# Spreading a chunk's row scatters over the steps of the expert blocks, in a causal-convolution and mixture-of-experts kernel on one core

## The chip, the cores and the metric

The kernel runs on one core of one Trainium2 chip. The core has five engines that run side by side and wait for each other by semaphores: TensorE (PE in the profile, with its weight loads as PEld), VectorE (DVE), ScalarE (ACT), GpSimd (POOL) and SyncE (SP, which here only issues transfers). Sixteen DMA engines move the data. The metric is the time of one execution on the device in microseconds (us).

## The reference

Two stages, one after the other, over 28672 tokens (8 sequences of 3584) of 192 numbers each:

```python
# 1: a causal filter of 7 taps, its weights a softmax, one filter for each of 8 groups of 24 columns
out = np.einsum('hk,bskhg->bshg', softmax(weight), x_unf)
x = out.reshape(28672, 192)

# 2: every token goes to the one expert of 8 that its direction fits best
logits = (x / |x|) @ (expert_emb / |expert_emb|).T / tau
e, gate = argmax(logits), its softmax probability
out[token] = gate * (np.maximum(x[token] @ w1[e], 0) @ w2[e])     # 192 -> 1024 -> 192
```

## The kernel before

The tokens are worked on in 16 **chunks** of 1792 (112 partitions by 16 columns). For a chunk, `mix` computes the filter on TensorE and the norms; `route` cuts the result into a high and a low half in 16 bits, transposes it by DMA (`turn`, L503), computes the logits and the expert of each token, and gives every token a place `di` in its expert's region of a table `rows_d` in DRAM. Then it writes the chunk's rows there with 16 indirect transfers of 112 rows, issued by GpSimd (`scatter`, L507), one for each column.

The experts' work is done in **blocks** of at most 512 tokens of one expert (`expert`, L653). SP loads a block's rows transposed (`fetch`, L632, up to three blocks ahead). VectorE copies the expert's weights into `slot` (L611 to L618). For each eighth of the hidden layer TensorE makes five matmuls into `h_ps` (L672), ScalarE writes the relu's high part (L674) and VectorE the low part (L675) into `hid`. Then, for each 128 tokens, 24 matmuls go into `o_ps` (L692), ScalarE scales the result by the gate into `y` (L696), and GpSimd scatters y to the output by token number (L697). `expert` is a generator: it yields once after each piece of the hidden layer and once after each y. These are the **steps**: twelve for a block of 512, eight and four.

`hand_out` makes blocks of the rows that are surely complete; it is called ahead of the chunks in `PICK` (2, 3, 5, 8, 12), and a block's loads wait for all scatters that had been issued by then (`need`). `last_blocks` does so at the end, after `pads` has scattered nine transfers of padding rows.

`dispatch` is a generator too: it runs `mix` and `route` of the chunks, up to two mixes ahead, and each yield states how much VectorE and ScalarE time it used. `run` ties the two together: after each step of a block it credits what VectorE and ScalarE have left beside TensorE (times `rate`, which `hand_out` sets so that the next hand-out comes `LEAD` before the blocks run out), and pulls pieces from `dispatch` while there is credit. Chunks 0 and 1 are worked on while the weights are prepared; chunks 2 to 15 run beside the blocks; after chunk 15 only blocks are left.

This order of the program is what the scheduler starts from. It orders the instructions of each engine by that priority and by when they are ready; SP alone keeps the written order. GpSimd executes its queue in order, and the scatters of a chunk and the y's of the blocks are in the same queue. The pools that touch them: `rows` has two buffers, `out` (y) four.

Of the kernel before, what the change touches and what calls it, by code (L numbers as in the profile page):

```python
# [16 lines left out]
AF = mybir.ActivationFunctionType  # L17
# [13 lines left out]
NT = 16  # L31
# [20 lines left out]
LEAD = 26.0  # L52

CAP = 6.0


def _dep(tc, frm, to, sync=True):
    cls = mybir.DependencyClass.Sync if sync else mybir.DependencyClass.NoSync
    tc.add_manual_dep(
        frm, to, mybir.DependencyInfo(cls, mybir.DependencyReason.DATA),  # L60
        reason="routed rows are written before they are read",
    )


class _Moe:
    def __init__(self, ctx, tc, x, weight, emb, tau, w1, w2, out):
        self.tc, self.nc = tc, tc.nc
        self.x, self.weight, self.emb, self.tau = x, weight, emb, tau
        self.w1, self.w2, self.out = w1, w2, out
        B, S, _ = x.shape  # L70
        self.B, self.S, self.N = B, S, B * S
        self.nch = self.N // CT
        self.per_b = S // CT
        self.cap = self.N + PAD
        self.dummy = E * self.cap
        pool = lambda name, bufs, **k: ctx.enter_context(
            tc.tile_pool(name=name, bufs=bufs, **k))
        self.cp = pool("const", 1)
        self.xp = pool("xload", 2)
        self.rp = pool("rows", 2)  # L80
        self.xtp = pool("xtrans", 2)
        self.sp = pool("small", 2)
        self.lp = pool("lone", 1)
        self.ep = pool("expert", 3)
        self.yp = pool("y", 3)
        self.op = pool("out", 4)
        self.mp = pool("meta", 8)
        self.rings = {k: pool("ps_" + k, n, space=PSUM)
                      for k, n in (("r", 2), ("l", 1), ("h", 5))}

        self.res = self.cp.tile([128, E * RES], F16, name="res")
        self.slot = self.cp.tile([128, S2 + RES - W2], F16, name="slot")
        self.hid = self.cp.tile([128, 2 * NFC * 512], F16, name="hid")
        self.dp = pool("scratch", 1, space=DRAM)
        self.rows_d = self.dp.tile([E * self.cap + PAD, RW], I32, name="rows_d")
        self.scatters = []
        self.xts, self.mixed = [], {}
        self.weights_in, self.later = False, []
        self.subs, self.ready, self.at, self.copied = [], 0, 0, 0
# [277 lines left out]
    def route(self, c, xbar):  # L377
        xTs = []
        nc, sp = self.nc, self.sp
        xc, s, si, f = self.mixed.pop(c)  # L380
        r32 = self.rp.tile([TP, NT, RW], I32, tag="rows", name="rows")
# [4 lines left out]
        for g in range(0, NT, GX):  # L386
# [7 lines left out]
                out=rows[:, u, 256:384], in0=xc[:, u, 0:128],  # L394
                in1=rows[:, u, 0:128], op=ALU.subtract)
            nc.vector.tensor_tensor(
                out=rows[:, u, 192:256], in0=xc[:, u, 128:192],
# [17 lines left out]
        for g in range(NT // GX):  # L415
            if xbar:
                xT = xTs[g]
            else:
                xT = self.xtp.tile([128, GX, 3, TP], F16, tag="xT", name="xT")
                for k in range(3):  # L420
                    tp = self.ps("r", [128, GX, TP], F16, "tr_ps")
                    for a in range(GX):
                        nc.tensor.transpose(
                            out=tp[:, a, :],
                            in_=rows[:, g * GX + a, k * 128:(k + 1) * 128],
# [3 lines left out]
            for a in range(GX):  # L429
                for k in range(3):  # L430
                    nc.tensor.matmul(  # L431
                        out=lg[:, g * GX + a, :], lhsT=xT[:, a, k, :],
# [7 lines left out]
            out=l, in_=lg.rearrange("p t (k e) -> p t e k", k=2), op=ALU.add,  # L440
# [3 lines left out]
        m = sp.tile([TP, NT], F32, tag="m", name="m")  # L444
# [12 lines left out]
            out=l, in0=l, scalar=0.0, op0=ALU.is_equal,  # L457
# [32 lines left out]
        self.dve = nc.vector.tensor_single_scalar(  # L490
            out=di, in_=dr, scalar=-1.0, op=ALU.add).ins
        yield 0.8, 0.0
        for t in range(NT):
            self.scatter(di[:, t:t + 1], r32[:, t, :])
            if t % 2:
                yield 0.3, 0.3
        self.left += CT


    def turn(self, rows, t, n):  # L500
# [152 lines left out]
    def expert(self):  # L653
        nc, tc = self.nc, self.tc
        while self.ready < min(self.at + 3, len(self.subs)):
            self.fetch()
        u, xT, mt, T = self.subs[self.at][3:]
        self.copy_w1(self.at)
        self.at += 1
        nj = T // 128  # L660
        w1 = lambda b, c: self.slot[:, b + c * 128:b + (c + 1) * 128]
        w2 = self.slot[:, S2:S2 + WS - W2].rearrange("p (c d) -> p c d", d=2 * D)
        hh, hl = (self.hid[:, i * NFC * T:(i + 1) * NFC * T].rearrange(
            "p (c t) -> p c t", t=T) for i in range(2))

        m = 512 // T
        for b in range(0, NFC, m):
            ps = self.ps("h", [128, m, T], F32, "h_ps")
            for c in range(m):
                for i, (o, k) in enumerate(  # L670
                        ((0, 0), (0, 2), (F, 0), (2 * F, 1), (3 * F, 1))):
                    nc.tensor.matmul(out=ps[:, c, :], lhsT=w1(o, b + c),  # L672
                                     rhs=xT[:, k, :], start=(i == 0), stop=(i == 4))
            nc.scalar.activation(out=hh[:, b:b + m, :], in_=ps, func=AF.Relu)  # L674
            nc.vector.scalar_tensor_tensor(  # L675
                out=hl[:, b:b + m, :], in0=ps, scalar=0.0, in1=hh[:, b:b + m, :],
                op0=ALU.max, op1=ALU.subtract)
            if b == (0 if m > 2 else 2 if m == 2 else 1) and u == 0:
                self.copy_w2()
            yield self.slack(512)  # L680
        self.copy_w1(self.at)

        g = self.yp.tile([128, 4], F32, tag="g", name="g")
        nc.vector.tensor_scalar(
            out=g[:, 0:nj], in0=mt[:, :, 1].bitcast(F32),
            scalar1=self.slot[:, S2 + WS - W2:S2 + WS - W2 + 2].bitcast(F32), scalar2=None, op0=ALU.mult)
        for a in range(nj):
            o = self.ps("h", [128, D], F32, "o_ps")
            q = slice(a * 128, (a + 1) * 128)
            for c in range(NFC):  # L690
                for i, (h, k) in enumerate(((hh, 0), (hh, D), (hl, 0))):
                    nc.tensor.matmul(out=o, lhsT=h[:, c, q], rhs=w2[:, c, k:k + D],  # L692
                                     start=(c + i == 0),
                                     stop=(c == NFC - 1 and i == 2))
            y = self.op.tile([128, D], F32, tag="y", name="y")
            nc.scalar.activation(out=y, in_=o, func=AF.Copy, scale=g[:, a:a + 1])  # L696
            i = nc.gpsimd.indirect_dma_start(  # L697
                out=self.out[:, :],
                out_offset=bass.IndirectOffsetOnAxis(ap=mt[:, a, 0:1], axis=0),
                in_=y, in_offset=None, bounds_check=self.N - 1,  # L700
                oob_is_err=False).ins
            tc.declare_no_dep(i, group="out", reason="tokens are distinct")
            tc.add_to_no_dep_group("out", i)
            yield OUT
# [16 lines left out]
    def dispatch(self, first, ring):  # L721
        a = b = ()
        na = nb = 0
        da = db = 0.0
        last = first if ring == "h" else self.nch
        share = AHEAD if ring == "h" else 1.0
        ca, cb = (0, 0) if ring == "h" else (first, first)
        a, b = None, None
        while cb < last:
            if b is None and cb in self.mixed:  # L730
                if ring != "h" and cb in PICK[1:]:
                    self.hand_out(cb)
                b, db = self.route(cb, ring != "h"), 0.0
            if a is None and ca < min(last, cb + 2):
                a, da = self.mix(ca, ring, first), 0.0
            if a is not None and (b is None or da * COST_B <= db * COST_A * share):
                v = next(a, None)
                if v is None:
                    a, ca = None, ca + 1
                    continue  # L740
                da += sum(v)
            else:
                v = next(b, None)
                if v is None:
                    b, cb = None, cb + 1
                    continue
                db += sum(v)
            yield v
# [25 lines left out]
    def run(self):  # L774
# [14 lines left out]
        a = self.dispatch(first, "h")  # L789
# [15 lines left out]
        a = self.dispatch(first, "r")  # L805
        for _ in range(PRE):
            next(a)
        live, due, done = next(a, None), [0.0, 0.0], False
        while live or not done or self.at < len(self.subs):
            if self.at < len(self.subs):  # L810
                for v in self.expert():
                    due = [min(CAP, d + self.rate * t) for d, t in zip(due, v)]
                    while live and min(due) >= 0.0:
                        due = [d - t for d, t in zip(due, live)]
                        live = next(a, None)
            elif live:
                live = next(a, None)
            if not live and not done:
                self.last_blocks()
                done = True  # L820
        order.__exit__(None, None, None)
# [19 lines left out]
```

## Time and profile before

| | |
|---|---|
| Median of 3 runs | 1531.99 us (1530.37 to 1540.09) |
| The profiled execution | 1535.34 us |
| Its span, first to last instruction | 1533.5 us |
| Mean granted clock of TensorE | 0.878 |
| Busy: PE, PEld, DVE, ACT, POOL | 1227.3, 917.6, 847.0, 575.5, 538.5 us |
| Indirect transfers on POOL: rows, y, padding | 256, 231, 9 |

Lines of the page and of the answers are read so: a group has its line in the kernel, engine, operation, what it writes and reads, and its count, then busy time and the mean in ns of one, then how long the engine stood idle just before these instructions and what ended most of that. A line with forty digits cuts the span into 40 slices of 38.3 us; a digit is the busy share in tenths, or for PEclk the clock that TensorE was granted. A line that begins with a stretch (200.90:234.90) gives its length and, for each engine, busy time and the count of instructions, then granted clock, the DMA engines' share and GB/s. A line of the timeline has start, duration, engine, line and operation, and in brackets the idle time before it and what ended that. "remote" and "another core or an unknown queue" stand for a semaphore whose update the profile could not put down to an instruction that ended near it. Ends of matmuls are modelled.

### The profile page before, as it was taken

The page shows a single profiled execution, that of the slowest core. Times are in us where ns is not written, and L with a number is a line of the kernel's source. Part 1 is how long each engine was busy: PE and PEld are TensorE (multiplying, and loading weights), DVE is VectorE, ACT ScalarE, POOL GpSimd, SP SyncE. Part 2 cuts the span into 40 slices and gives each one's busy share as a digit, 9 for nine tenths or more (in the row PEclk, how much of TensorE's full clock was granted, in tenths as well). Part 3 has the DMA queues.
Part 4 walks back from the last instruction along what each step waited for, and adds up shares of the span by engine and source line. Part 5 has one row for each costly group of instructions (what it writes and reads, how often), then busy time and mean ns, then how long its engine had stood idle before and what let it go on. Part 6 is the DMA issues. An engine that isn't in the chain of part 4 may idle for free.

```text
span 1533.5 us, 28412 instructions
## 1 busy us (share of the span) xinstructions
PE 1227.3 (80%) x10460; PEld 917.6 (60%) x10460; DVE 847.0 (55%) x2162; ACT 575.5 (38%) x1335; POOL 538.5 (35%) x564
## 2 busy tenths in 40 slices
PE   4745768877968677798696969595899999998997
PEld 2533647665647454455473647373577767778787
DVE  3945857656537456375562627253555465547745
ACT  3834525524342323353343325131333333333332
POOL 0044255355343433533524242526222222222222
PEclk9656979878879788797898979797899999999999
DMA  9334463455315254254362523332122112211210
GB/s 257 103 102 137 101 141 94 94 125 125 82 47 119 55 130 105 77 126 102 79 132 57 124 66 61 78 61 77 32 53 48 43 35 49 53 37 41 56 37 24
DMA packets 273228, 129.07 MB, mean 84 GB/s; under 512 B 215054, under 2 KB 263565, under 8 KB 273088
## 3 DMA queue, kind: packets, MB, share of 16 engines
q1 hardware_dynamic: 249280, 80.39, 24.7%
q0 software_dynamic: 23808, 46.87, 10.1%
q8 instruction: 82, 1.34, 0.4%
q14 instruction: 58, 0.48, 0.1%
HBM read 38.35 MB, written 47.53 MB: 56 GB/s over the span
## 4 chain that ended last, share of the span: by engine, by line
PE 62%; another core or an unknown queue 9%; issue 7%; DVE 4%; ACT 3%; DMA 3%; SPq 2%; POOL 0%; POOLq 0%; DVEq 0%; ACTq 0%
PE h_ps L672 28%; PE o_ps L692 28%; PE conv_ps L344 5%; ACT hid L674 2%; SPq L503 2%; PE lg_ps L431 2%; DMA xT<-rows 2%; DMA xt<-in_dram 2%; DVE hid L675 1%; DVE slot L617 1%; ACT sq L354 1%; ACT rows L391 0%; DVE slot L611 0%; ACT xt L347 0%
## 5 line engine op out<-in xcount | busy, mean ns | idle before, releaser
L692 PE MATMUL o_ps<-slot,hid 128*128 128x192 f16 x5544 | 546.7, 255 | 155.9 <-issue 94.7
L692 PEld LDWEIGHTS <-hid 128*128 128x128 f16 x5544 | 479.3, 101 | 218.9 <-issue 144.7
L672 PE MATMUL h_ps<-e_xT,slot 128*128 128x512 f16 (+2 forms) x3520 | 556.5, 312 | 46.5 <-DVE hid L675 29.5
L697 POOL DMA_INDIRECT out_dram<-y,e_mt x231 | 259.0, 1121 | 728.2 <-ACT y L696 654.3
L675 DVE SCALAR_TENSOR_TENSOR hid<-h_ps,hid 128x512 f16<-128x512 f32 x462 | 313.5, 687 | 296.6 <-ACT hid L674 215.0
L672 PEld LDWEIGHTS <-slot 128*128 128x128 f16 x3520 | 311.8, 100 | 240.3 <-issue 70.7
L674 ACT ACTIVATE hid<-h_ps 128x512 f16<-128x512 f32 x462 | 271.1, 597 | 430.4 <-PE h_ps L672 236.7
L507 POOL DMA_INDIRECT rows_d<-rows,di x256 | 258.0, 1008 | 181.9 <-issue 99.8
L696 ACT ACTIVATE y<-o_ps,g 128x192 f32<-128x192 f32 x231 | 91.4, 419 | 342.9 <-PE o_ps L692 212.7
L617 DVE COPY slot<-res 128x3074 f16 x82 | 79.9, 975 | 185.5 <-PE o_ps L692 110.7
L344 PE MATMUL conv_ps<-xt,band 128*112 128x384 f32 x256 | 116.7, 567 | 39.9 <-DMA xt<-in_dram 35.0
L347 ACT COPY xt<-conv_ps 112x384 f32<-112x384 f32 x128 | 60.8, 479 | 116.1 <-PE conv_ps L344 84.8
L611 DVE COPY slot<-res 128x3072 f16 x82 | 78.5, 958 | 40.6 <-remote 37.0
L431 PEld LDWEIGHTS <-xT 128*112 128x112 f16 x768 | 67.6, 149 | 47.1 <-DMA xT<-rows 17.1
L344 PEld LDWEIGHTS conv_ps<-xt,band 128*112 128x112 f32 x256 | 45.7, 202 | 63.5 <-issue 44.9
L431 PE MATMUL lg_ps<-ma,xT 128*112 128x16 f16 x512 | 67.0, 202 | 18.3 <-DMA xT<-rows 11.5
L354 ACT ACTIVATE sq<-xt 112x192 f32<-112x192 f32 x192 | 67.9, 356 | 4.8 <-DVE sq L357 2.3
L389 DVE TENSOR_TENSOR xt<-xt,x_p_s 112x768 f32<-112x768 f32 x64 | 58.2, 950 | 0.0
L431 PE MATMUL lg_ps<-mb,xT 128*112 128x16 f16 x256 | 50.1, 206 | 8.7 <-ACT xT L427 5.7
L391 ACT CAST rows<-xt 112x768 f16<-112x768 f32 x64 | 50.6, 829 | 12.2 <-DVE xt L389 7.5
L357 DVE SCALAR_TENSOR_TENSOR sq<-xt 112x192 f32<-112x192 f32 x64 | 22.6, 354 | 57.5 <-ACT sq L354 56.6
L393 DVE TENSOR_TENSOR rows<-xt,rows 112x512 f16<-112x512 f32 x64 | 43.6, 682 | 2.1 <-DMA out_dram<-y,e_mt 1.2
(157 smaller groups left out, 543.3 us busy)
## 6 DMA issues: line engine op xcount, KB each, us to landing
xt<-in_dram SPq DMA_DIRECT2D x8, 1536.0 KB
xt<-in_dram SPq DMA_DIRECT2D x8, 1440.0 KB
rows_d<-rows,di POOLq DMA_INDIRECT x256
out_dram<-y,e_mt POOLq DMA_INDIRECT x231
xT<-rows SPq DMA_TRANSPOSE x224
hid<-in_dram SPq DMA_DIRECT2D x3, 768.0 KB
slot<-in_dram SPq DMA_DIRECT2D x3, 768.0 KB
hid<-in_dram SPq DMA_DIRECT2D x3, 512.0 KB
```

Source lines behind the costliest of these rows:

```text
L344: nc.tensor.matmul(out=ps, lhsT=self.band[:, h, :], rhs=xt[:, :, h * G:(h + 1) * G], start=True, stop=True)
L354: nc.scalar.activation(out=sq, in_=xc[:, t, :], func=AF.Square, accum_out=n2[:, t:t + 1])
L431: nc.tensor.matmul(out=lg[:, g * GX + a, :], lhsT=xT[:, a, k, :], rhs=self.mb if k == 1 else self.ma, start=(k == 0), stop=(k == 2))
L507: i = self.nc.gpsimd.indirect_dma_start(out=self.rows_d[:, :], out_offset=bass.IndirectOffsetOnAxis(ap=idx, axis=0), in_=src, in_offset=No ...
L611: nc.vector.tensor_copy(out=self.slot[:, 0:W2], in_=v)
L617: self.nc.vector.tensor_copy(out=self.slot[:, S2:], in_=self.res[:, bass.ds(self.we + W2, RES - W2)])
L672: nc.tensor.matmul(out=ps[:, c, :], lhsT=w1(o, b + c), rhs=xT[:, k, :], start=(i == 0), stop=(i == 4))
L674: nc.scalar.activation(out=hh[:, b:b + m, :], in_=ps, func=AF.Relu)
L675: nc.vector.scalar_tensor_tensor(out=hl[:, b:b + m, :], in0=ps, scalar=0.0, in1=hh[:, b:b + m, :], op0=ALU.max, op1=ALU.subtract)
L692: nc.tensor.matmul(out=o, lhsT=h[:, c, q], rhs=w2[:, c, k:k + D], start=(c + i == 0), stop=(c == NFC - 1 and i == 2))
L696: nc.scalar.activation(out=y, in_=o, func=AF.Copy, scale=g[:, a:a + 1])
L697: i = nc.gpsimd.indirect_dma_start(out=self.out[:, :], out_offset=bass.IndirectOffsetOnAxis(ap=mt[:, a, 0:1], axis=0), in_=y, in_offset=No ...
```

## The change

`route` no longer issues a chunk's scatters. It appends the 16 of them to a list, `pend`, and the main loop issues them with `put`: after two of every three steps of the blocks one scatter, with a dependency on the step's ScalarE instruction (the relu of L674 or the y of L696). There are exceptions. Ahead of a hand-out, `dispatch` puts out all that is pending, without a dependency. After the last chunk, one goes out after each step, also without one, and `last_blocks` comes when none is left. In the chunks 0 and 1, worked on with the weights, the scatters go out in `route` as before. A new route is begun only while at most 16 scatters are pending; until then `dispatch` yields a piece of 0.5 without work, if it has no mix to do either.

```diff
+SPREAD = 3
...
         yield 0.8, 0.0
-        for t in range(NT):
-            self.scatter(di[:, t:t + 1], r32[:, t, :])
-            if t % 2:
-                yield 0.3, 0.3
+        self.pend += [(di[:, t:t + 1], r32[:, t, :]) for t in range(NT)]
+        while self.pend and not xbar:
+            self.put()
+            yield 0.15, 0.15
         self.left += CT
+
+
+    def put(self, step=None):
+        if self.pend:
+            self.scatter(*self.pend.pop(0))
+            if step is not None:
+                _dep(self.tc, self.scatters[-1], step.name)
...
-            nc.scalar.activation(out=hh[:, b:b + m, :], in_=ps, func=AF.Relu)
+            self.step = nc.scalar.activation(
+                out=hh[:, b:b + m, :], in_=ps, func=AF.Relu).ins
...
-            nc.scalar.activation(out=y, in_=o, func=AF.Copy, scale=g[:, a:a + 1])
+            self.step = nc.scalar.activation(
+                out=y, in_=o, func=AF.Copy, scale=g[:, a:a + 1]).ins
...
-            if b is None and cb in self.mixed:
+            if b is None and cb in self.mixed and len(self.pend) <= NT:
                 if ring != "h" and cb in PICK[1:]:
+                    while self.pend:
+                        self.put()
+                        self.put()
+                        yield 0.3, 0.3
                     self.hand_out(cb)
...
+            elif b is None:
+                v = 0.5, 0.5
             else:
...
-        live, due, done = next(a, None), [0.0, 0.0], False
-        while live or not done or self.at < len(self.subs):
+        live, due, done, steps = next(a, None), [0.0, 0.0], False, 0
+        while live or self.pend or not done or self.at < len(self.subs):
             if self.at < len(self.subs):
                 for v in self.expert():
+                    steps += 1
+                    if not live and not done:
+                        self.put()
+                    elif steps % SPREAD:
+                        self.put(self.step)
...
-            elif live:
-                live = next(a, None)
-            if not live and not done:
+            else:
+                self.put()
+                if live:
+                    live = next(a, None)
+            if not live and not done and not self.pend:
                 self.last_blocks()
                 done = True
```

More of the change, by code (lines that the diff above doesn't have):

```diff
@@ L95, in __init__ @@
         self.rows_d = self.dp.tile([E * self.cap + PAD, RW], I32, name="rows_d")
-        self.scatters = []
+        self.scatters, self.pend, self.step = [], [], None
         self.xts, self.mixed = [], {}
```

## The prediction, made before the change was run

> **What bounds the kernel now.** I read the slices of the page first, then its groups, then windows of busy time laid around each chunk's scatters.
>
> ```profile
> PE   4745768877968677798696969595899999998997
> POOL 0044255355343433533524242526222222222222
> PEclk9656979878879788797898979797899999999999
> ...
> PE 62%; another core or an unknown queue 9%; issue 7%; DVE 4%; ACT 3%; DMA 3%; SPq 2%; POOL 0%; POOLq 0%; DVEq 0%; ACTq 0%
> ...
> L692 PE MATMUL o_ps<-slot,hid 128*128 128x192 f16 x5544 | 546.7, 255 | 155.9 <-issue 94.7
> L672 PE MATMUL h_ps<-e_xT,slot 128*128 128x512 f16 (+2 forms) x3520 | 556.5, 312 | 46.5 <-DVE hid L675 29.5
> L697 POOL DMA_INDIRECT out_dram<-y,e_mt x231 | 259.0, 1121 | 728.2 <-ACT y L696 654.3
> L507 POOL DMA_INDIRECT rows_d<-rows,di x256 | 258.0, 1008 | 181.9 <-issue 99.8
> ```
>
> TensorE (PE) carries the kernel: the blocks' matmuls at L692 and L672 are 1103 of its 1227 us. From slice 29 on, where no chunk is left, it is full at full clock. Before that its digits and the granted clock dip where POOL's digit rises. So I laid 34 us windows from the first scatter of each chunk. These are the nine chunks (3, 5, 6, 8, 9, 10, 12, 13, 14) whose scatters the change gates; columns are length, then busy time of PE, its weight loads, DVE, ACT and POOL, then granted clock, DMA share and GB/s.
>
> ```profile
> 250.30:284.30 34.00, 23.23 (x197) 17.44 (x195) 16.51 (x43) 8.04 (x21) 22.50 (x22) 0.85 0.63 151
> 359.10:393.10 34.00, 22.70 (x156) 15.91 (x154) 15.75 (x44) 9.09 (x28) 18.57 (x18) 0.75 0.55 134
> 413.20:447.20 34.00, 20.58 (x111) 11.19 (x109) 8.35 (x13) 6.63 (x13) 19.39 (x20) 0.75 0.26 72
> 560.70:594.70 34.00, 19.16 (x137) 12.44 (x136) 10.74 (x27) 11.15 (x37) 19.06 (x20) 0.75 0.23 62
> 621.80:655.80 34.00, 22.66 (x145) 14.07 (x144) 10.60 (x27) 9.52 (x36) 20.06 (x22) 0.70 0.24 69
> 680.30:714.30 34.00, 25.73 (x167) 16.65 (x166) 16.01 (x43) 10.29 (x36) 21.05 (x22) 0.75 0.31 86
> 801.70:835.70 34.00, 20.01 (x118) 11.80 (x117) 8.05 (x14) 8.21 (x16) 18.06 (x20) 0.80 0.27 65
> 873.90:907.90 34.00, 19.33 (x109) 11.49 (x107) 8.11 (x17) 5.98 (x13) 19.05 (x20) 0.75 0.29 78
> 964.80:998.80 34.00, 17.23 (x94) 9.36 (x92) 5.72 (x10) 5.33 (x11) 19.25 (x20) 0.66 0.30 74
> sum 306.00, PE 190.62 PEld 120.36 DVE 99.84 ACT 74.24 POOL 176.98; mean PE 21.18 PEld 13.37 DVE 11.09 ACT 8.25 POOL 19.66
> ```
>
> The thirteen stretches between the bursts (their sum, and one of them) and the block-only tail look quite different:
>
> ```profile
> 393.10:413.20 20.10, 20.10 (x169) 14.30 (x168) 15.69 (x40) 10.40 (x21) 4.95 (x7) 1.00 0.21 37
> sum 396.80, PE 384.74 PEld 294.47 DVE 291.63 ACT 200.72 POOL 86.61; mean PE 29.59 PEld 22.65 DVE 22.43 ACT 15.44 POOL 6.66
> 1100.00:1500.00 400.00, 382.39 (x3761) 301.65 (x3759) 225.17 (x387) 138.33 (x270) 102.65 (x95) 1.00 0.20 46
> ```
>
> Between bursts PE is busy 384.74 of 396.80 us (97%), with the same mixing and routing beside the blocks; in the tail 96%. Nearly all that PE loses in the middle of the kernel, it loses while a chunk's 16 scatters run. That no engine's own work causes this shows in the timeline of chunk 14's burst:
>
> ```profile
> 960.57 8.08 PE L692 MATMUL o_ps<-slot,hid 128*128 128x192 f16 x96
> ...
> 976.01 0.94 POOL L507 DMA_INDIRECT rows_d<-rows,di  x1 [0.30 <-DMA rows_d<-rows,di]
> 977.94 1.01 DVE L617 COPY slot<-res 128x3074 f16 x1 [13.90 <-remote]
> 977.99 0.42 ACT L696 ACTIVATE y<-o_ps,g 128x192 f32<-128x192 f32 x1 [10.60 <-remote]
> ```
>
> The last of these matmuls should have ended at 968.65, yet the copy of w2 and the fourth y, which both wait for it, start together at 977.9, DVE having stood for 13.90 us. Meanwhile POOL issues without a stop: 0.94 us and 0.30 of idle, one scatter in 1.24 us. PE's completions come late as long as POOL runs back to back. By what path one holds up the other no row tells.
>
> The Trainium skill, SBUF — State Buffer, section "Who interferes with whom", states that PE and ACT never wait on anyone. By it the scatters could not hold PE and spreading them would give nothing; the late release at 977.9 does not agree, but it is counted as a rival below.
>
> **What the change does, and the price of the gap.** Sixteen scatters a chunk no longer go out at once: in two of three steps (a relu or a y) one goes, and it waits for that step's ACT instruction. No transfer is removed or added; the waits are semaphore instructions of 17 ns on POOL (shortest and median; the longest is a real wait). Five bursts stay: those flushed ahead of the hand-outs (chunks 2, 4, 7, 11; the first and the last are shown), and chunk 15 with the nine pad scatters, which nothing gates. I take no gain there.
>
> ```profile
> L507 POOLq EVENT_SEMAPHORE  x18: 17/17/11480, 102.6 to 1045.9; - x18
> ...
> 200.90:234.90 34.00, 21.64 (x141) 14.48 (x141) 15.16 (x53) 6.97 (x20) 21.02 (x21) 0.65 0.54 135
> 733.70:767.70 34.00, 21.60 (x147) 14.77 (x146) 18.13 (x77) 12.47 (x39) 19.77 (x21) 0.80 0.34 82
> 1039.70:1089.70 50.00, 25.78 (x169) 16.77 (x167) 15.34 (x75) 6.24 (x12) 30.03 (x32) 0.66 0.18 60
> ```
>
> The gain is what the nine windows lose against a full PE. Idle time alone: 306.00 - 190.62 = 115 us. With the clock: window minus busy times granted clock gives 14.3, 17.0, 18.6, 19.6, 18.1, 14.7, 18.0, 19.5 and 22.6, together 162 us, which spreads the half clock evenly over idle and busy time. If all of the half clock fell on busy time, it would be 115 plus the sum of (1 - clock) x 34 over the nine rows, 76, so 191. I take 150, nearer to the even spread but below it, since part of the half clock lies on idle time. That is 1.04 us for each of 144 scatters.
>
> **What a spread scatter still costs.** Nothing in the trace of before runs gated. Below, it could be zero: in 393.10:413.20 POOL issues seven transfers in 20.10 us and PE is full. Less than zero I exclude, since a scatter gives PE no work sooner. Above, it is the 1.04 us of the burst. The nearest row is inside chunk 4's burst, where DVE's copies stretched the scatters:
>
> ```profile
> 314.50:322.00 7.50, 7.04 (x52) 5.95 (x52) 3.29 (x11) 2.04 (x4) 5.97 (x5) 0.62 0.46 108
> 322.00:331.50 9.50, 4.07 (x34) 2.52 (x32) 0.99 (x7) 0.16 (x1) 6.87 (x8) 0.76 1.08 256
> ```
>
> At five scatters in 7.5 us, 1.5 us apart, PE is back to 7.04 of 7.50; when they close up again to seven transfers in 9.5 us (with the x load beside them), it falls to 4.07. So density decides, not the count. I take 0.46 / 5 = 0.09 us a scatter, 13 us for 144.
>
> How dense will they be? From 200.9 to 1039.7 thirteen chunks take 838.8 us, 64.5 each; less 17 lost (150 / 9) that is 47.5. In it POOL has 16 scatters and about nine y's (130 of the 231 y's lie before 1089.7):
>
> ```profile
> 0.00:1089.70 1089.70, 147.03 (x130) 0.83 0.42 101
> ...
> 1089.59 8.63 PE h_ps L672 x40
> 1098.23 7.92 PE o_ps L692 x96
> ```
>
> 25 x 1.24 = 31 us of 47.5, 65% against 100% in a burst. A block of 512 is eight steps of 1.08 us and four of 1.98, 16.55 in all; 16 scatters need 24 steps, two blocks, 33 us of PE, and with the chunk's own matmuls between them about the whole chunk. On average a scatter every 2.9 us, a transfer of any kind every 1.9.
>
> **Queues.** Behind a waiting scatter on POOL stand the next y's transfer, which needs a later ACT step anyway, and the clearing of the next chunk's rows (L383), which may start up to a few steps later; ACT's cast into rows would feel that, and hides it behind relus. SP's loads of blocks name only scatters that a flush has put out before. With the stalls gone, next in line is what the stretches between bursts show: 3% idle, late x loads among it. On the 156 us left of the nine windows that is 5 us.
>
> Sum against the profiled execution's 1535.3 us: 1535.3 - 150 + 13 + 5 = 1403. The median of the runs, 1532.0, lies 3.3 below it; so **1400 us**.
>
> **Rivals.**
> 1. *The o steps are still too dense* (0.18). There a y and two thirds of a scatter go out per 1.98 us: 6.7 x 1.24 = 8.3 us of POOL in 7.92 of PE. If each such stretch acts like the end of a burst, its last three transfers hold PE, about 4 us; 2 blocks x 9 chunks x 4 = 72 us back: 1472. For it: the row 322.00:331.50. Against: the tail runs four y's in a row with a full PE, and the chunk's matmuls stretch these steps.
> 2. *Nothing changes* (0.07): each scatter costs its 1 us wherever it stands, or the steps waited for have passed when POOL arrives and the burst stays: 1532. Against: 314.50:322.00.
> 3. *Hand-outs come late* (0.07). A route now waits while over 16 scatters are pending. From 560.7 to 733.7 three chunks take 173 us, less 17 each 41, about 20 steps at 47.5 / 24; 16 scatters need 24. The hand-outs at 12 and, less, at 5 slip by up to 20 us; if the blocks run dry, 40 us: 1440.
> 4. *Slower* (0.07). Small stalls all through the gated chunks keep the clock at half, where now only a third of each chunk suffers. Nine chunks hold 9 x 47.5 = 428 us of PE at full clock. At the lowest mean clock seen, 0.66, they take 648; now they take 9 x 64.5 = 580. That is 68 more: 1600. It decides against the change below a mean clock of 428 / 580 = 0.74. Against: the clock is 1.00 in most stretches between bursts.
>
> The Trainium skill, TensorE: Matmul & The Clock Gate, section "What's actually happening", gives the gate as half rate after an idle window of about 3.4 us and full rate after a busy one. By that rule gaps of a microsecond would not bring rival 4 about, and its chance would be below 0.07; 314.50:322.00, at 0.62 with PE 94% busy just after a stall, shows only the return.
>
> **How the numbers follow.** My forecast has 0.61 and reaches from 1355 (the 191 all gained, a little left) to 1450. With rivals 1 and 3 taken in, the range is 1355 to 1490 and leaves out rivals 2 and 4 and the edges, about 0.2. A measurement of this kernel can tell about 1% (15 us) from no change. Faster by more: forecast and rivals 1 and 3, 0.86; same, rival 2, 0.07; slower, rival 4, 0.07.
>
> **What would show it.** In the new profile the scatters stand singly or in pairs on POOL; the clock's digits are 9 except at five places; the share "another core or an unknown queue" in the chain, which is where the late releases are put, falls to about a third; PE's busy time in windows over gated chunks is above 90%. The prediction is wrong if PE's gaps follow the gated scatters one by one, if the clock stays near 0.7, or if PE stands before a hand-out for lack of blocks.

## The result and the profile after

| | before | after |
|---|---|---|
| Median | 1536.04 us (4 runs, 1530.37 to 1542.93) | 1454.82 us (4 runs, 1453.44 to 1458.41) |
| Profiled execution, its span | 1535.34, 1533.5 us | 1455.95, 1454.2 us |
| Mean granted clock | 0.878 | 0.909 |

The ratio is 0.947 (0.942 to 0.952): faster by 81 us, where 132 had been foretold. In the changed kernel the scatter stands in L515, the indices `di` in L491, h_ps in L680, its relu in L682, o_ps in L701, y in L705 and the transfer of y in L707. Its page:

```profile
PE   4744877869888688787899998759999999999997
POOL 0045243474455344555344535542221222222222
PEclk9656978989999799897999999869999999999999
...
PE 45%; DVE 3%; issue 3%; another core or an unknown queue 3%; SPq 1%; DMA 1%; ACT 1%; POOL 0%; POOLq 0%; DVEq 0%; ACTq 0%
...
L680 PE MATMUL h_ps<-e_xT,slot 128*128 128x512 f16 (+2 forms) x3520 | 561.8, 312 | 65.0 <-issue 42.8
L701 PE MATMUL o_ps<-slot,hid 128*128 128x192 f16 x5544 | 526.9, 251 | 76.8 <-issue 54.6
L515 POOL DMA_INDIRECT rows_d<-rows,di x256 | 266.9, 1043 | 204.1 <-issue 75.9
```

PE's idle time ahead of o_ps has halved, from 155.9 to 76.8 us, and the share of late releases in the chain fell from 9% to 3%. But the idle time ahead of h_ps grew from 46.5 to 65.0, and the digits show more than the five dips foretold. The windows of 34 us from the first scatter of the same nine chunks (length, then busy PE, PEld, DVE, ACT, POOL, then clock, DMA share, GB/s), the first, the best and the sum:

```profile
248.60:282.60 34.00, 25.73 (x207) 19.05 (x205) 20.28 (x55) 9.19 (x22) 22.31 (x20) 0.90 0.62 151
...
803.10:837.10 34.00, 33.19 (x257) 22.34 (x255) 12.60 (x30) 17.18 (x52) 20.90 (x21) 1.00 0.31 78
...
sum 306.00, PE 256.21 PEld 180.96 DVE 157.73 ACT 110.89 POOL 186.60; mean PE 28.47 PEld 20.11 DVE 17.53 ACT 12.32 POOL 20.73
```

PE is busy 84% of them, against 62% before. What the gated chunks still lose is seen on POOL in the first of these windows, and on PE beside it:

```profile
248.64 0.93 POOL L515 DMA_INDIRECT rows_d<-rows,di  x1 [0.30 <-DVE di L491]
249.87 0.93 POOL L515 DMA_INDIRECT rows_d<-rows,di  x1 [0.30 <-issue]
...
261.53 0.93 POOL L515 DMA_INDIRECT rows_d<-rows,di  x1 [0.30 <-issue]
264.80 1.53 POOL L707 DMA_INDIRECT out_dram<-y,e_mt  x1 [2.33 <-ACT y L705]
...
280.43 0.93 POOL L515 DMA_INDIRECT rows_d<-rows,di  x1 [0.99 <-ACT hid L682]
```

```profile
251.87 0.24 PE L701 MATMUL o_ps<-slot,hid 128*128 128x192 f16 x1 [0.50 <-issue]
252.59 0.24 PE L701 MATMUL o_ps<-slot,hid 128*128 128x192 f16 x1 [0.48 <-issue]
253.33 0.24 PE L701 MATMUL o_ps<-slot,hid 128*128 128x192 f16 x1 [0.49 <-issue]
254.88 0.24 PE L701 MATMUL o_ps<-slot,hid 128*128 128x192 f16 x1 [1.31 <-issue]
```

The first scatter is released by `di`, and nine follow with 0.30 us between them. Nine of these ten carry no wait for ScalarE at all in the trace; that a y ahead of them in POOL's queue already waits for a later step is argued from the program, not shown. While they run, PE starts matmuls singly. Of the 144 gated scatters 92 carry such a wait, and few were held by it, as POOL's waits for a row scatter show (total, times, longest):

```profile
POOL rows_d L515 <- DVE di L491: 61.1, 5, 42.8
POOL rows_d L515 <- ACT hid L682: 39.8, 24, 4.0
```

For the comparisons below two numbers are worked out from the traces. **Lost**: for each of the chunks 2 to 15, the time from its first scatter to that of the next chunk (30 us past the last scatter for chunk 15), less PE's busy time in it weighted by the granted clock. **Dense gaps**: pairs of neighbouring row scatters of one chunk that start less than 1.5 us apart; transfers of y are not counted, and 1.5 is a line drawn for the count, not a limit that a run has found. Before: 269.6 us lost, 167.4 of them in the nine chunks; 184 dense gaps, 119 in the nine. After: 189.6 and 84.0; 126 and 64. The five bursts that were to stay lose 102 us before and 106 after.

### The profile page after: what moved, and what is told of

It reads as the page before. It is cut to its first block, busy times and chain, and to the rows that moved or that the text cites. A ratio compares the mean times of both kernels' runs of the same rounds, so it can differ in the third digit from the quotient of the medians.

```text
span 1454.2 us, 28516 instructions
## 1 busy us (share of the span) xinstructions
PE 1207.1 (83%) x10460; PEld 906.0 (62%) x10460; DVE 843.9 (58%) x2162; ACT 573.3 (39%) x1335; POOL 554.2 (38%) x564
## 4 chain that ended last, share of the span: by engine, by line
PE 45%; DVE 3%; issue 3%; another core or an unknown queue 3%; SPq 1%; DMA 1%; ACT 1%; POOL 0%; POOLq 0%; DVEq 0%; ACTq 0%
PE h_ps L680 22%; PE o_ps L701 21%; PE conv_ps L345 1%; SPq L511 1%; DVE slot L625 1%; DMA xT<-rows 1%; DVE hid L684 1%; ACT hid L682 1%; PE lg_ps L432 1%; DVE slot L619 0%; DVE xt L390 0%; POOL out_dram L707 0%; DVE slot L622 0%; DVE rows L394 0%
## 5 line engine op out<-in xcount | busy, mean ns | idle before, releaser
L680 PE MATMUL h_ps<-e_xT,slot 128*128 128x512 f16 (+2 forms) x3520 | 561.8, 312 | 65.0 <-issue 42.8
L701 PE MATMUL o_ps<-slot,hid 128*128 128x192 f16 x5544 | 526.9, 251 | 76.8 <-issue 54.6
L701 PEld LDWEIGHTS <-hid 128*128 128x128 f16 x5544 | 470.9, 100 | 124.9 <-issue 84.6
L707 POOL DMA_INDIRECT out_dram<-y,e_mt x231 | 265.8, 1150 | 596.5 <-ACT y L705 548.0
L680 PEld LDWEIGHTS <-slot 128*128 128x128 f16 x3520 | 312.1, 100 | 269.3 <-issue 93.6
L682 ACT ACTIVATE hid<-h_ps 128x512 f16<-128x512 f32 x462 | 268.7, 597 | 376.4 <-PE h_ps L680 244.7
L515 POOL DMA_INDIRECT rows_d<-rows,di x256 | 266.9, 1043 | 204.1 <-issue 75.9
L705 ACT ACTIVATE y<-o_ps,g 128x192 f32<-128x192 f32 x231 | 91.9, 419 | 339.5 <-PE o_ps L701 226.1
L345 PE MATMUL conv_ps<-xt,band 128*112 128x384 f32 x256 | 111.6, 546 | 40.4 <-DMA xt<-in_dram 34.6
```

What stands on the lines that cost most here:

```text
L345: nc.tensor.matmul(out=ps, lhsT=self.band[:, h, :], rhs=xt[:, :, h * G:(h + 1) * G], start=True, stop=True)
L515: i = self.nc.gpsimd.indirect_dma_start(out=self.rows_d[:, :], out_offset=bass.IndirectOffsetOnAxis(ap=idx, axis=0), in_=src, in_offset=No ...
L680: nc.tensor.matmul(out=ps[:, c, :], lhsT=w1(o, b + c), rhs=xT[:, k, :], start=(i == 0), stop=(i == 4))
L682: self.step = nc.scalar.activation(out=hh[:, b:b + m, :], in_=ps, func=AF.Relu).ins
L705: self.step = nc.scalar.activation(out=y, in_=o, func=AF.Copy, scale=g[:, a:a + 1]).ins
L707: i = nc.gpsimd.indirect_dma_start(out=self.out[:, :], out_offset=bass.IndirectOffsetOnAxis(ap=mt[:, a, 0:1], axis=0), in_=y, in_offset=No ...
```

## The experiments

The runs were made on four chips, each with the kernel before beside them. The chips were not alike:

| chip | kernel before |
|---|---|
| the first measurements | 1536.04 us (4 runs) |
| 14 (e1 to e4) | 1327.72 us (7 runs, 1325.0 to 1330.18) |
| 6 (e5 to e8) | 1536.1 us (13 runs, 1525.61 to 1549.52) |
| 5 (e9 to e11) | 1330.17 us (13 runs, 1324.48 to 1332.89) |
| 10 (e12) | 1533.57 us (8 runs, 1525.33 to 1536.24) |

The same program has two times, some 205 us apart, by where it ran. The expectations of e1 to e4 were written before that was known.

**e1 and e2: the kernel before, with 9 or 4 small memsets on POOL behind each scatter**, which keep a burst's scatters apart (shown with `PAUSES` as in e2, without the dependencies that hold the order):

```diff
+PAUSES = 4
...
+        self.idle = self.cp.tile([128, 8], F32, name="idle")
...
         self.scatters.append(i)
+        for _ in range(PAUSES):
+            p = self.nc.gpsimd.memset(self.idle, 0.0).ins
```

> The kernel before, with nine small memsets (0.1 us each) on GpSimd behind every row scatter, so that a chunk's scatters stand about 2.15 us apart by themselves, with no wait for any step, in all bursts, pads too. Theory density (PE's completions are held back only while POOL issues transfers back to back, 1.24 us apart, for more than about five): the bursts of chunks 2 to 15 stop holding PE, of about 270 us lost some 200 come back: 1310 to 1390. Theory count (each row scatter costs PE about 1 us wherever it stands): 1536 or a little over. Theory memory traffic (the stall comes from the rows' writes): a burst has the same bytes over 35 us instead of 20, gain under half: about 1440 to 1536.

> The same with four memsets: scatters about 1.65 us apart. Theory density with a limit between 1.25 and 1.5 us a transfer: nearly the gain of nine memsets, 1310 to 1400. If the limit lies near 2 us: half of that gain, about 1440. Theory count: 1536.

Measured on chip 14: e1 1539.29 us, ratio 1.158 (1.155 to 1.161); e2 1381.43 us, ratio 1.040 (1.038 to 1.043). Both are slower, and nothing was there to be won. What the pauses cost shows in what PE waits for, first of e1 (total, times, longest), then in the group of e2:

```profile
PE h_ps L681 <- DMA e_xT<-rows_d: 179.4, 6, 46.6
```

```profile
L681 PE MATMUL h_ps<-e_xT,slot 128*128 128x512 f16 (+2 forms) x3520 | 549.4, 310 | 49.2 <-DMA e_xT<-rows_d 48.0
```

These are the blocks' loads: they wait for all scatters issued ahead of their hand-out, which now end later, and the blocks run dry.

**e3: the change, with gated scatters held back until 14 steps after their route**, meant to leave no scatter waiting for a step that has passed (the lines that count the steps in `self.since` are left out).

```diff
+LAG = 14
...
-                    elif steps % SPREAD:
+                    elif steps % SPREAD and (
+                            len(self.pend) > NT or self.since >= LAG):
```

> The changed kernel, but a chunk's gated scatters begin only 14 steps after its route has been put down, so that the steps they wait for have not passed yet when the indices are ready. Theory clumps (what is left of the stalls in the nine gated chunks, 84 us, comes from the 6 to 17 transfers that run back to back at the start because their steps are past): clumps go, some 45 us come back: 1395 to 1430. Theory count (0.5 us for each gated scatter): 1455. Rival: the later end of the scatters delays routes and hand-outs: 1455 to 1500.

Measured on chip 14: 1397.25 us, ratio 1.052 (1.050 to 1.055). A later start alone costs. The largest loss, 40.3 us, follows chunk 11, ahead of the last hand-out: there PE has no block to work on from 679 to 719 us. The clumps stayed in large part (51 dense gaps in the nine chunks), and on this chip the run could not have shown what they cost.

**e4 and e8: the change without its waits**; the scatters keep their places in the program.

```diff
-                        self.put(self.step)
+                        self.put()
```

> The changed kernel without the waits: the scatters are put at the same places of the program, but none waits for a step. Theory wait: the scheduler puts them out as soon as the indices are ready, 16 in a row again: 1520 to 1550, the time of before. Rival (the place in the program order suffices): 1455.

> The change without its waits: scatters are put out at the same places of the program, but wait for no step. If the waits carry the gain on a stalling chip (the kernel before at 1536 us): about 1536 us there, ratio 1.00. If the places in the program carry it: 1455 us, ratio 0.947. On a chip where the kernel before takes 1328 us: 1339 us as in e4, ratio 1.008.

Measured on chip 14 (e4): 1339.16 us, ratio 1.008 (1.005 to 1.011). On chip 6 (e8): 1549.29 us, ratio 1.011 (1.008 to 1.013). So where the kernel before takes 1536 us, the waits carry the whole gain, and the moved places none of it. This pair is also the cleanest look at the stall: one program, two chips. The windows of the nine chunks, e8 first, then e4, one chunk (13) and the sum of each:

```profile
857.30:891.30 34.00, 17.20 (x109) 10.17 (x108) 2.58 (x5) 4.44 (x9) 19.34 (x22) 0.70 0.38 88
...
sum 306.00, PE 180.75 PEld 110.92 DVE 91.51 ACT 64.60 POOL 177.77; mean PE 20.08 PEld 12.32 DVE 10.17 ACT 7.18 POOL 19.75
```

```profile
731.00:765.00 34.00, 33.35 (x279) 23.93 (x277) 15.28 (x35) 18.51 (x52) 24.92 (x26) 1.00 0.42 101
...
sum 306.00, PE 272.02 PEld 203.66 DVE 177.27 ACT 137.40 POOL 214.30; mean PE 30.22 PEld 22.63 DVE 19.70 ACT 15.27 POOL 23.81
```

With the same burst on POOL and a DMA share no higher, PE makes 109 matmuls on chip 6 and 279 on chip 14. PE's timeline in that burst, e8, then e4:

```profile
867.00 0.32 PE L701 MATMUL o_ps<-slot,hid 128*128 128x192 f16 x1 [1.80 <-issue]
867.73 0.32 PE L701 MATMUL o_ps<-slot,hid 128*128 128x192 f16 x1 [0.41 <-issue]
869.15 0.32 PE L701 MATMUL o_ps<-slot,hid 128*128 128x192 f16 x1 [1.09 <-issue]
871.49 0.32 PE L701 MATMUL o_ps<-slot,hid 128*128 128x192 f16 x1 [2.02 <-issue]
873.59 0.32 PE L701 MATMUL o_ps<-slot,hid 128*128 128x192 f16 x1 [1.78 <-issue]
875.68 0.32 PE L701 MATMUL o_ps<-slot,hid 128*128 128x192 f16 x1 [1.78 <-issue]
```

```profile
737.47 2.32 PE L680 MATMUL h_ps<-e_xT,slot 128*128 128x512 f16 x10
...
748.09 4.12 PE L701 MATMUL o_ps<-slot,hid 128*128 128x192 f16 x48
```

On chip 6 single matmuls of 0.32 us start up to 2.3 us apart, every 2.1 us at the end, with no wait that the profile shows ("issue"); on chip 14 they run without a gap. PE's idle time of this kind over the whole kernel (total, times, longest), all rows above 3 us of e8, then the only one of e4:

```profile
PE h_ps L680 <- issue: 83.4, 57, 11.6
PE o_ps L701 <- issue: 54.6, 50, 2.6
PE lg_ps L432 <- issue: 26.8, 37, 2.0
```

```profile
PE conv_ps L345 <- issue: 2.8, 1, 2.8
```

In all, e8 loses 283.8 us over 166 dense gaps and e4 99.2 over 144. Hardly any of what e4 loses is such idle time: its waits name a load, transposed rows, ScalarE or VectorE.

**e5 and e6: the kernels before and after, unchanged, on chip 6.**

> The kernel before, unchanged, for a trace on the same chip as the three runs below. The prediction's theory (a burst of scatters 1.24 us apart delays TensorE's completions, as a property of the kernel): 1536 us, windows over the bursts lose 270 us of PE in chunks 2 to 15. Rival (the delay belongs to the chip on which the first profiles were taken, since this kernel took 1328 us in the first four experiments): where it takes about 1328 us, the trace shows the same bursts of 16 scatters about 1.2 us apart and loses only about 100 us in chunks 2 to 15; where it takes about 1536 us, both theories say 270.

> The change, unchanged. Prediction's theory: ratio 0.947 on every chip, since the burst's cost goes with the kernel. Rival (the cost goes with the chip): where the kernel before takes about 1536 us the ratio is again 0.947; where it takes about 1328 us there is nothing to gain and the waits cost what they cost against the same kernel without them (1339 us there): between e4's 1339 and e3's 1397, I take 1365, ratio 1.028.

Measured: e5 1548.3 us in its one run; e6 1462.03 us, ratio 0.949 (0.942 to 0.956). The first result comes again, with the same marks: 289.9 us lost before, 206.1 after, and 184 and 125 dense gaps.

**e7: the change, with the chunks ahead of hand-outs and the last one gated too**; a hand-out waits until its scatters are out.

```diff
-            if b is None and cb in self.mixed and len(self.pend) <= NT:
-                if ring != "h" and cb in PICK[1:]:
-                    while self.pend:
-                        self.put()
-                        self.put()
-                        yield 0.3, 0.3
+            hand = ring != "h" and cb in PICK[1:]
+            if b is None and cb in self.mixed and len(self.pend) <= (
+                    0 if hand else NT):
+                if hand:
...
-                    if not live and not done:
-                        self.put()
-                    elif steps % SPREAD:
+                    if steps % SPREAD:
```

> The change, and the four chunks ahead of hand-outs and the last chunk are gated too (the hand-out waits until the chunk's scatters are out). Theory of bursts: on a chip that stalls, four to five bursts of 18 to 21 us lost become 8 to 11 each, minus 40 us against the change, if the hand-outs lose nothing by coming 30 us later; theory that hand-outs set the end: each of the three later hand-outs costs up to 30 us, plus 30 to 60 us. On a chip where the kernel before takes 1328 us only the second acts: slower than the change by 30 to 60 us.

Measured on chip 6: 1448.0 us, ratio 0.942 (0.935 to 0.948), 14 us below e6 (1442.54 to 1451.17 against 1452.71 to 1465.66), where 40 were expected: the five chunks still have 39 of 63 dense gaps, and the stretch from chunk 11's first scatter to chunk 12's, past the hand-out, grew from 78.5 us in e6 to 91.2 in e7 with little more work in it (past the hand-out PE waits 8.7 us for a block's load). e6, then e7:

```profile
676.20:754.70 78.50, 61.93 (x471) 43.43 (x469) 45.68 (x143) 30.74 (x73) 32.10 (x36) 0.87 0.37 93
```

```profile
687.00:778.20 91.20, 63.83 (x472) 42.20 (x470) 42.79 (x117) 29.34 (x59) 29.51 (x35) 0.83 0.38 92
```

**e9: the change, unchanged, on chip 5.**

> The change, unchanged, for a chip on which it has not been timed. Where the kernel before takes about 1536 us: 0.947 to 0.949 as twice measured. Where it takes about 1328 us, theory that only the bursts' stall is spared: nothing to spare, and the waits delay scatters and with them the hand-outs of expert work, between e4 (1339, no waits) and e3 (1397, waits and a later start): I take 1365, ratio 1.028. Rival there (the waits are free): 1339, ratio 1.008.

Measured: 1326.91 us, ratio 0.999 (0.997 to 1.001). My 1365 was wrong: the waits as they stand are free, the rival's answer and better. Scatters are in clumps here too (119 dense gaps in chunks 2 to 15), and PE does not mind. Its page and its nine windows:

```profile
PE 42%; issue 3%; DVE 2%; DMA 2%; POOL 1%; ACT 1%; SPq 1%; DVEq 0%; POOLq 0%; ACTq 0%
...
L701 PE MATMUL o_ps<-slot,hid 128*128 128x192 f16 x5544 | 504.7, 249 | 12.3 <-DVE slot L625 5.5
```

```profile
sum 306.00, PE 283.53 PEld 209.51 DVE 188.91 ACT 135.52 POOL 211.76; mean PE 31.50 PEld 23.28 DVE 20.99 ACT 15.06 POOL 23.53
```

No share for late releases is left in the chain, and 12.3 us of idle time ahead of o_ps. 86.6 us are lost in chunks 2 to 15, 42.5 of them in the nine.

**e10 and e12: the 4 memsets once more; e11: the 4 memsets in the change.**

> The kernel before with four small memsets on POOL behind each scatter, so that bursts run about 1.65 instead of 1.24 us apart (it took 1381 us where the kernel before took 1328). Where the kernel before takes about 1536 us: by the prediction's density claim (late at 1.24 us, free at 1.5 us) the stall is gone and the time is again about 1381 us, ratio 0.90. Rival (each scatter costs TensorE about 0.6 us however far apart, which is what the spread scatters of the change still cost): the stall stays and the pauses come on top, about 1536 + 54 = 1590 us, ratio 1.035. Where the kernel before takes 1328 us: ratio 1.04 again.

> The change with the same four memsets behind each scatter, so that the clumps at the start of a gated chunk and the five bursts that stay run 1.65 us apart as well. Where the kernel before takes about 1536 us: if the clumps' density is what the spread chunks still lose (84 us in nine chunks) and what the five bursts lose (107 us), some 60 and 60 us of these go and pauses give back about 20: 1462 - 100 = 1360 us, ratio 0.885. Rival (the loss goes with the number of scatters): 1462 to 1480 us, ratio 0.95 to 0.965. Where it takes about 1328 us: 10 to 30 us over the change.

> The kernel before with four memsets behind each scatter (issues about 1.65 instead of 1.24 us apart in a burst), once more, for a chip on which the kernel before takes about 1536 us. There: if only bursts 1.24 us apart stall TensorE and 1.5 us is free, the time is that of the chips without the stall, 1382 us, plus at most 20: ratio 0.90 to 0.913. Rival, each scatter costs TensorE about 0.6 us at any distance: lost in chunks 2 to 15 falls from 290 to 224 x 0.6 = 134 us, but the 54 us that the pauses cost elsewhere come back: about 1536 - 156 + 54 = 1434 us, ratio 0.93. Rival, the stall doesn't depend on the distance at this scale: 1590 us, ratio 1.035. Where the kernel before takes about 1328 us: ratio 1.04, and nothing new.

e10 and e11 ran on chip 5: 1381.72 us, ratio 1.038 (1.036 to 1.040), and 1369.89 us, ratio 1.029 (1.026 to 1.031), 43 us over e9 where 10 to 30 were expected. They repeat e2: without a stall pauses only cost. What pauses in the change give on a chip that stalls was not run. e12 ran on chip 10, where the kernel before takes 1533.57 us: **1393.19 us, ratio 0.907** (0.903 to 0.910), inside the 0.90 to 0.913 that "1.24 stalls, 1.5 is free" had named, and outside both rivals. POOL in it, its chain and its nine windows:

```profile
795.09 0.95 POOL L509 DMA_INDIRECT rows_d<-rows,di  x1
796.04 0.61 POOL L520 MEMSET idle<- 128x8 f32 x4
796.79 0.95 POOL L509 DMA_INDIRECT rows_d<-rows,di  x1
```

```profile
PE 30%; DVE 3%; POOL 3%; issue 2%; ACT 1%; DMA 0%; DVEq 0%; ACTq 0%; another core or an unknown queue 0%; POOLq 0%; SPq 0%
```

```profile
sum 306.00, PE 275.61 PEld 196.88 DVE 181.10 ACT 131.60 POOL 249.74; mean PE 30.62 PEld 21.88 DVE 20.12 ACT 14.62 POOL 27.75
```

The same 256 scatters, 1.70 us apart instead of 1.24, with no dense gap: PE is busy 90% of the windows, the late releases are gone from the chain, and 127.5 us are lost in chunks 2 to 15, no more than on the chips without a stall (131.3 in e10, 134.1 in e2). A little of the stall is left: PE's idle time with "issue" adds up to 12.7 us, against 2.6 in e10, and the run is 11 us longer than that one.

Setting what a kernel loses on a stalling chip against what the same kernel loses on one without, per dense gap: the change (189.6 or 206.1 - 86.6) / 126 or 125 = 0.82 or 0.96 us; without waits (283.8 - 99.2) / 166 = 1.11 us; with pauses no gap is left, and next to no loss. As an estimate from these runs, **on such chips each pair of row scatters as close as in a burst costs PE about 1 us**, and what the change is worth is the number of pairs that it opens. Spacings between 1.24 and 1.70 us were not tried one by one.

For chips that stall the plain pauses are the best that was run (0.907 on chip 10, against 0.942 for e7 and 0.949 for the change on chip 6); on the others they cost 4% and the change nothing. Nothing that was run beat the kernel before on chips 5 and 14.

## Why the prediction was right, and where it was off

**The range held in part by luck.** The 1454.8 us measured lie inside 1355 to 1490, but 5 us beyond the 1450 to which the forecast itself was to reach. The room above that had been made for rivals 1 and 3, and neither of them is the main cause of the shortfall. And on chip 5 the same change gives 0.999: that there was a gain to foretell hung on where the kernel ran.

**What bounds the kernel: right where the stall exists.** Every view that the prediction read (dips of PE under POOL's peaks, releases by "remote") is there in e5 and e8. It took them for the kernel's own, though, and that was unfounded: on chips 5 and 14 such bursts bring no stall (2.8 us of "issue" in e4 and in e9). Its words "completions come late" are too narrow as well. e8's timeline shows matmuls that start late one by one.

**Density, not count: right.** It rested on one window, 314.50:322.00. e12 shows it for 256 scatters. The Trainium skill, SBUF — State Buffer, section "Who interferes with whom", lets PE wait on no one, in a section on SBUF's ports. e4 and e9 agree with that (272.02 and 283.53 of 306 us busy under the bursts), e8 does not (180.75), unless the burst acts there by another path than those ports; by which, no row says.

**The gain in the nine windows, 150 us: too much.** It set them against a full PE, and so counted ordinary waits as stall. The nine chunks lose 54 us in e4 and 42.5 in e9 without a stall, by waits for loads, for the transposed rows, for ACT and DVE. Of the 167.4 us lost before, the stall is thus 113, if the kernel before has the ordinary waits of e4. Two of its windows (chunks 12 and 13) begin 1.3 and 3.8 us ahead of the first scatter; moved there, they give the same sum for PE, 190.62. That 113 is near the 115 at the lower end of the step is chance: idle time alone holds ordinary waits too.

**13 us for the scatters that were spread, and 5 for ordinary waits: too little.** The nine chunks still lose 84.0 us: 42.5 as in e9 without a stall, in place of 5, and 41.5 of stall, in place of 13. The second is the step that failed. "How dense will they be" was answered with a mean, a scatter every 2.9 us, by dividing a chunk's time by its scatters. The program ties a scatter to a step that stands ahead of it in the program; if `di` comes later than that, the step has passed, and the wait is void (52 of the 144 carry none at all). A relu held only 24 scatters, and of the 119 dense gaps in the nine chunks 64 stay; the longest run of transfers without a pause is 6 to 17 in each chunk. This is the second half of rival 2 ("the steps waited for have passed when POOL arrives and the burst stays"), for about half of the close pairs. The 150 - 13 - 5 = 132 us foretold thus became 167.4 - 84.0 = 83.4, against 81 measured.

**Five bursts stay: right**, 102 and 106 us.

**The queues: right.** e9 shows that the waits delay nothing that counts (0.999).

**The rivals.** Rival 1 put what is left into the o steps. The longest row of scatters alone (ten in chunk 3, quoted above) stands at the chunk's start instead, where the indices come. But the longest run of transfers, 17 in chunk 9 from 575.88 to 597.47 us, mixes 13 scatters with four y's, and from 592 us PE starts o_ps matmuls singly in it; so a part of rival 1 is not ruled out. Rival 3, late hand-outs, did not come with the change (PE waits 5.2 us in all for blocks' loads), but it is real: e1, e2, e3 and, in part, e7 pay it. Rival 4 fell: the clock rose from 0.878 to 0.909. The half clock that it feared is real, though. In e8 the granted clock is 0.50 from 870 to 878 us, among the single matmuls shown above, and PE stands no longer than 2.02 us at a time there. The prediction held that gaps of a microsecond would not bring this about; gaps of two did.

**What would show it.** The share of late releases fell to a third, as said. PE above 90% in the windows came in two of nine; scatters singly or in pairs, and digits of 9 except at five places, did not come. Of the signs of being wrong, a clock near 0.7 and a PE without blocks ahead of a hand-out did not come either.

## What to carry to other kernels

A dip of one engine under another's burst is a fact of the trace, and not yet of the program: run the kernel on a second chip before tuning against it, since here some 205 us hung on where it ran. Before pricing such a dip, subtract what the same stretch loses without it. And a wait on a step spreads work only if the step comes after the data: ask of each wait added which of its two sides is ready last, and count the spacing of neighbours, not the mean.

## What the runs showed of the hardware that was not expected

The kernel before takes 1328 and 1330 us on two chips and 1534 and 1536 us on two others, each steady within 2% over 7 to 13 runs. Chip 6 differs from 14 in the same program (e8, e4) by PE's starts, down to one per 2.1 us under a burst of scatters 1.24 us apart.

The traces differ in one more thing. An indirect transfer mostly shows 16 updates of its semaphore where the record is nearly full (457 of the 496 in e10), so 496 x 16 = 7936 are to be looked for in a run. The traces hold 7670 of these events on chip 14 (e4) and 7784 on chip 5 (e10), but 3213 on chip 6 (e8), and on chip 10 still only 4565 in e12, in which next to nothing stalls. So the two kinds of chip differ in how such events pass or are recorded even almost without a stall. Whether that is the cause, and whether it lies in the chip, in the core or in what else was running beside it, stays open.
